# One filter product per unit on GpSimd, weight conversion wholly on VectorE, a conversion operation behind each filter unit, and the next item's stages one step later

## The chip, the cores and the metric

One core of a Trainium2 chip. The metric is the device time of one execution in microseconds (us), the median over several executions. PE is TensorE, DVE is VectorE, ACT is ScalarE, POOL is GpSimd, SP is SyncE, which only issues transfers here. L391 and the like are source lines; the changed kernel's lines stand up to 15 further down than the same lines before (the products of the plain steps are L609 before and L624 after).

## The reference

```python
X = np.fft.rfft(x, axis=1)                    # x: (8, 3008, 256)
Y = X * (filt_r + 1j * filt_i)[None]
y = np.fft.irfft(Y, n=3008, axis=1)           # then 24064 tokens of 256
h = y.reshape(24064, 256) @ w_in              # 256 -> 2048
g = h * np.clip(h + 3.0, 0.0, 6.0) / 6.0
out = g @ w_out                               # 2048 -> 256
```

The line that makes `g` is called the hardswish here.

## The kernel before

The transforms are written as matmuls in stages, and the feed-forward part as steps over blocks of 512 tokens, eight steps a block. From the second block on each product is done with seven instead of eight sub-products, which needs sums of weight blocks. The beginning has four stretches: loading and the first stage of batch item 0; its filter stage; the "direct" stage, which makes the first tokens; and the eight *plain steps* of the first block, which do without the weight sums. In the plain steps the weights are also converted: they are read as 64-bit words and turned into fp32 by integer and float operations, in 16 parts of 128x512, eleven of them within the plain steps, each shortly before the product that needs it. Some steps also hold a few *token products*, which make the tokens of a later stretch, and the first stage of batch item 1 runs beside the steps.

One filter unit, three products on VectorE:

```python
def f_unit(b, i):                       # cut
    if near(b, i):                      # b == 1, or b == 0 and i == NU - 2
        ...                             # four half products
    else:
        nc.vector.tensor_tensor(out=s1, in0=ps, in1=f, op=ALU.mult)
        nc.vector.tensor_tensor(out=s2[re], in0=ps[re], in1=f[im], op=ALU.mult)
        nc.vector.tensor_tensor(out=s2[im], in0=ps[im], in1=f[re], op=ALU.mult)
```

One conversion: six operations on VectorE, beside ScalarE's absolute value, and an end on VectorE (one operation) or on GpSimd (two):

```python
def w_conv(i, last):                    # cut
    v.tensor_scalar(out=big, in0=hi, ...)
    v.scalar_tensor_tensor(out=big, in0=hi, scalar=top_c, in1=big, ...)
    v.tensor_scalar(out=rest, in0=big, ...)
    v.tensor_scalar(out=lo, in0=lo, ...)
    v.scalar_tensor_tensor(out=rest, in0=lo.bitcast(FP32), scalar=1.0, in1=rest, ...)
    v.scalar_tensor_tensor(out=rest, in0=rest, scalar=2.0 ** -20, in1=big, ...)
    if last is v:
        v.scalar_tensor_tensor(out=w_part(i)[1], in0=two(high), scalar=least, in1=two(rest), ...)
    else:                               # GpSimd
        last.tensor_scalar(out=high, in0=high, scalar1=least, scalar2=None, op0=ALU.is_ge)
        last.tensor_tensor(out=w_part(i)[1], in0=two(high), in1=two(rest), op=ALU.mult)
```

The first stage of batch item 1 runs beside the steps. Its result goes through a pool of two buffers and is stored by SyncE for item 1, by GpSimd for later items; a block's output is stored by SyncE too, at the end of a step:

```python
t1p = pool("t1p", 2)
...
for c, s in enumerate(a_at):            # item 1: steps 2 to 9
    at(s, a_unit, n, c)                 # products; ScalarE copies them to a t1p buffer
    at(s, z_store, n, c, nc.sync if n == 1 else nc.gpsimd)
```

Of the kernel before, what the change touches and what calls it, by code (L numbers as in the profile page):

```python
# [10 lines left out]
FP32 = mybir.dt.float32  # L11
I32 = mybir.dt.int32
AXT = mybir.ActivationFunctionType
ALU = mybir.AluOpType
# [13 lines left out]
P = 128  # L28
# [6 lines left out]
NB = HC // XC  # L35
# [5 lines left out]
NU = KH // 2  # L41
# [73 lines left out]
def kernel(  # L115
# [9 lines left out]
    nc = tc.nc  # L125
# [14 lines left out]
    def pool(name, bufs, **kw):  # L140
        return ctx.enter_context(tc.tile_pool(name=name, bufs=bufs, **kw))
# [9 lines left out]
    rp = pool("rp", 2)  # L151
# [3 lines left out]
    op = pool("op", 2)  # L155
# [44 lines left out]
    def w_part(i):  # L200
        p = i // 2
        if i % 2 == 0:
            cols = ts(p, 256)
            src = moe_w_in[:, cols].bitcast(I32)
            return src.rearrange("(a p) d -> p a d", p=P), w_in[p][:, 0:4, :].rearrange("p (a j) m -> p a (j m)", a=2)
        src = moe_w_out[ts(p, 2 * P), :].bitcast(I32)
        return src.rearrange("(a p) d -> p a d", p=P), w_out[p][:, 0:4, :].rearrange("p (a j) m -> p a (j m)", a=2)
# [21 lines left out]
    def w_abs(i):  # L229
        words = st["bits", i].rearrange("p (n two) -> p n two", two=2)  # L230
        st["high", i] = sp.tile([P, 512], FP32, name="s1")
        nc.scalar.activation(out=st["high", i], in_=words[:, :, 1].bitcast(FP32), func=AXT.Abs)


    def w_conv(i, last):
        words = st.pop(("bits", i)).rearrange("p (n two) -> p n two", two=2)
        lo, hi = words[:, :, 0], words[:, :, 1]
        big, rest = (yp.tile([P, 2, D], FP32, name="y").bitcast(I32).rearrange("p a n -> p (a n)") for j in range(2))
        v = nc.vector
        high = st.pop(("high", i), None)  # L240
        v.tensor_scalar(out=big, in0=hi, scalar1=3, scalar2=0x3FFFFFFF,
                        op0=ALU.logical_shift_left, op1=ALU.bitwise_and)
        v.scalar_tensor_tensor(out=big, in0=hi, scalar=top_c, in1=big,
                               op0=ALU.bitwise_and, op1=ALU.bitwise_or)
        v.tensor_scalar(out=rest, in0=big, scalar1=23, scalar2=23,
                        op0=ALU.logical_shift_right, op1=ALU.logical_shift_left)
        v.tensor_scalar(out=lo, in0=lo, scalar1=9, scalar2=0x3F800000,
                        op0=ALU.logical_shift_right, op1=ALU.bitwise_or)
        if high is None:
            v.tensor_scalar(out=hi, in0=hi, scalar1=1, scalar2=1,  # L250
                            op0=ALU.logical_shift_left, op1=ALU.logical_shift_right)
            high = hi.bitcast(FP32)
        rest, big = rest.bitcast(FP32), big.bitcast(FP32)
        v.scalar_tensor_tensor(out=rest, in0=lo.bitcast(FP32), scalar=1.0, in1=rest,
                               op0=ALU.subtract, op1=ALU.mult)
        v.scalar_tensor_tensor(out=rest, in0=rest, scalar=2.0 ** -20, in1=big, op0=ALU.mult, op1=ALU.add)

        least = 1.125 * 2.0 ** -15
        two = lambda t: t.rearrange("p (a d) -> p a d", a=2)
        if last is v:  # L260
            v.scalar_tensor_tensor(out=w_part(i)[1], in0=two(high), scalar=least, in1=two(rest), op0=ALU.is_ge, op1=ALU.mult)
        else:
            last.tensor_scalar(out=high, in0=high, scalar1=least, scalar2=None, op0=ALU.is_ge)
            last.tensor_tensor(out=w_part(i)[1], in0=two(high), in1=two(rest), op=ALU.mult)

    def w_sums(i, late):
        w = (w_in, w_out)[i % 2][i // 2]
# [41 lines left out]
    def zt(dh):  # L309
        return (xn.rearrange("p a n -> p (a n)"), xs.rearrange("p i j d -> p (i j d)"))[dh]  # L310

    def copy(dve, to, ps):
        if dve:
            nc.vector.tensor_copy(out=to, in_=ps)
        else:
            nc.scalar.activation(out=to, in_=ps, func=AXT.Copy)
# [10 lines left out]
    def turn(c):  # L327
        t = t2p.tile([P, TC, D], FP32, name="t2")
        for v in range(2):
            ps = psU.tile([P, 512], FP32, name=("al", "be")[v])  # L330
            for u in range(2):
                for dh in range(2):
                    k = c * TC + 2 * v + u
                    nc.tensor.transpose(ps[:, ds(u * D + dh * P, P)], zt(dh)[:, ts(k, P)], st["start"][:, 0:P])
            copy(c == 0 and v == 1, t[:, 2 * v:2 * v + 2, :].rearrange("p k d -> p (k d)"), ps)
        st["t2", 0, c] = t
# [43 lines left out]
    def f_unit(b, i):  # L380
        c, r = divmod(2 * i, TC)
        ps = st.pop(("ps", b, i))
        f = st["ft", b, c][:, r:r + 2, :]

        pool_, n1, n2 = (hp, "h0", "h1") if b == 0 and i & 2 else (sp, "s1", "s2")
        s1, s2 = (pool_.tile([P, 512], FP32, name=n).rearrange("p (u d) -> p u d", u=2) for n in (n1, n2))

        re, im = slice(0, HALF), slice(HALF, P)
        if near(b, i):
            for s, part, to, x_ in (s1, re, re, re), (s1, re, im, im), (s2, im, re, im), (s2, im, im, re):  # L390
                nc.vector.tensor_tensor(out=s[to], in0=ps[x_], in1=f[part], op=ALU.mult)  # L391
        else:
# [3 lines that stand above are left out]
        st["y", b, i] = s1, s2  # L396


    def near(b, i):
        return b == 1 or b == 0 and i == NU - 2  # L400

    def y_unit(b, i):
        s1, s2 = st["y", b, i]
# [44 lines left out]
    for b in range(B):  # L448
        j = 0
        while j < HC:  # L450
            n = 1 if b == 0 and j == NJ else min(NJ, HC - j)
# [236 lines left out]
    with tc.manual_schedule():  # L688
# [22 lines left out]
        def convert(n):  # L711
            nonlocal done
            for i in range(n):
                w_conv(done, nc.vector)
                done += 1


        def convert_one():
            nonlocal done
            w_abs(done)  # L720
            w_conv(done, nc.gpsimd)
            done += 1
            load_bits(NCONV)

# [2 lines left out]
        ps = psU.tile([P, 512], FP32, name="al")  # L727
        for i in range(2):
            nc.tensor.matmul(ps, zero[:, P:2 * P], zero, start=True, stop=True)
        for j, n, bits in (0, 4, 0), (4, 4, 1), (8, 8, 1), (16, 8, 1), (24, 4, 1), (28, 4, 1):  # L730
            x0_load(j, n)
            load_bits(bits)
        table_load(0, 0)
# [9 lines left out]
        last = x0_at(HC * D - 2048, 3 * ND)  # L743
# [4 lines left out]
        nc.sync.dma_start(wai[:, 0:8, :], wai_d[:, 0:8, :])  # L748
        load_bits(4)
        turn(0)  # L750
        for c in range(NT):
            for i in (2 * c, 2 * c + 1):
                b_unit(0, i)
                f_unit(0, i)
                if c == NT - 1:
                    y_unit(0, i)
            if c + 1 < NT:
                turn(c + 1)
            if c:
                bi_unit(0, 2 * c - 2)  # L760
                (g0_first if c == NT - 1 else lambda i: g_store(0, i))(2 * c - 2)
            if c == 4:
                t4_load(0, 0, KH - 3 * TC, 1)
        t4_load(0, KH - 3 * TC, KH - TC, 1)
        for i in 1, 2:
            w_abs(i)
        direct(NU - 2)
        direct(NU - 1)
# [3 lines left out]
        bi_unit(0, NU - 2)  # L772
        for i in NU - 4, NU - 2:
            g_store(0, i)
        for i in 3, 4:
            w_abs(i)
        convert(4)
        for i in range(1, done):
            w_sums(i, False)

# [2 lines left out]

        at(0, x_load, 1, 0)

        for i, s in enumerate((0, 0, 1, 2, 2, 3, 4, 4, 5, 5, 6)):
            at(s, convert_one)
            at(s + 1, w_sums, done + i, False)
        for p in range(NP):
# [24 lines left out]
        def places(n):  # L814
            k = first[n]
            u = [NU - 1 - i for i in range(NU)]
            b_at = [(k - 2 - j // 3) * NP + 6 - 2 * (j % 3) for j in u]

            bi_at = [b_at[i] + (5 if i % 6 == 1 else 3) for i in range(NU)]
            a_at = [(k - 7 + c // 4) * NP + (0, 2, 5, 7)[c % 4] for c in range(NB)]  # L820
            if n == 1:
                a_at = list(range(2, NB + 2))
                b_at = [12, 13, 14, 18, 19, 20, 21, 22, 26, 27, 28, 29]
                bi_at = [i + 3 for i in b_at]
            return a_at, b_at, bi_at

        prev = None
        for n in range(1, B):
            a_at, b_at, bi_at = places(n)
# [7 lines left out]
            for c in range(NT):  # L837
                s = b_at[2 * (c - TB) + 1] + 1 if c >= TB else a_at[-1] + 1
                at(s, t2_load, n, c)
                s = b_at[2 * (c - FB) + 1] + 1 if c >= FB else a_at[-1 if n > 1 else 3] + 1  # L840
# [13 lines left out]
        for i in range(len(items) + 1):  # L854
            up = i < len(items)
            k, p = items[min(i, len(items) - 1)]
# [54 lines left out]
        k, v, add = NBLK - 1, nc.vector.tensor_tensor, ALU.add  # L911
# [37 lines left out]
```

## Time and profile before

| us | before |
|---|---|
| median of 4 runs | 2744.39 us (2740.41 to 2745.24) |
| span of the profiled run | 2739.3 us |
| filter products of the second pair start | 32.22 |
| first product of the plain steps | 69.74 |
| first product of the second block | 148.72 |
| a first-stage product of item 3 | 726.71 |

The last four rows are marks for a ledger. The filter products come in six *pairs* of units; a pair's start is its first product on TensorE. The profile of before is of one of its quicker runs (2741.46 us), which is why differences of 1 to 3 us are taken from runs of one chip together, and the profiles are used for where time goes.

### The profile page before, as it was taken

How to read it: one execution, taken by the hardware profiler on the slowest of the kernel's cores; microseconds unless marked ns; L12 is line 12 of the kernel's file. 1: busy time of each engine (PE TensorE's matmuls, PEld its weight loads, DVE VectorE, ACT ScalarE, POOL GpSimd, SP SyncE). 2: the span in 40 equal slices, each digit the busy share in tenths (PEclk: the TensorE clock that was granted, in tenths of full speed). 3: DMA queues.
4: the chain of work that ended last, by engine and by line, in shares of the span. 5: the costliest groups of instructions: out<-in, count | busy, mean ns of one | idle time of the engine just before them, and what ended most of it. 6: DMA issues, size and time to landing. Idle time of an engine off the chain costs nothing.

```text
span 2739.3 us, 47106 instructions
## 1 busy us (share of the span) xinstructions
PE 2701.9 (99%) x18100; PEld 2404.1 (88%) x18100; DVE 1955.4 (71%) x3383; ACT 1329.9 (49%) x2662; POOL 458.8 (17%) x646
## 2 busy tenths in 40 slices
PE   8899999999999999999999999999999999999998
PEld 6578889998899988999889998899988999999997
DVE  6868766787567875678756777577775777766665
ACT  3344455445544455444554445544455454545443
POOL 2833321101210012100121001210012100100000
PEclk9999999999999999999999999999999999999999
DMA  8642233221332123321233212332123321100000
GB/s 233 182 114 85 50 86 90 73 56 47 87 92 74 50 55 87 89 69 50 56 92 101 65 39 61 90 95 69 39 57 91 92 73 39 43 23 24 19 9 16
DMA packets 119644, 195.87 MB, mean 72 GB/s; under 512 B 21561, under 2 KB 82681, under 8 KB 119105
## 3 DMA queue, kind: packets, MB, share of 16 engines
q1 hardware_dynamic: 101627, 148.14, 19.1%
q0 software_dynamic: 17152, 44.23, 6.9%
q8 instruction: 143, 2.34, 0.4%
q14 instruction: 80, 0.66, 0.1%
q10 hardware_dynamic: 642, 0.51, 0.1%
HBM read 120.86 MB, written 71.93 MB: 70 GB/s over the span
## 4 chain that ended last, share of the span: by engine, by line
PE 93%; DVE 3%; DMA 2%; POOL 1%; issue 1%; ACT 0%; SPq 0%; POOLq 0%; DVEq 0%
PE po L598 42%; PE al L522 23%; PE be L522 17%; PE psn L476 4%; PE psf L376 3%; PE psf L353 2%; PE psf L423 2%; DVE s L391 1%; PE po L620 1%; DMA w_all<-in_x_dram 1%; DMA xs<-in_x_dram 0%; DVE g L572 0%; PE al L609 0%; DVE g L579 0%; PE po L376 0%
## 5 line engine op out<-in xcount | busy, mean ns | idle before, releaser
L598 PEld LDWEIGHTS po<-w_all,g 128*128 128x128 f32 x10304 | 1368.2, 191 | 142.1 <-issue 38.1
L598 PE MATMUL po<-w_all,g 128*128 128x128 f32 x10304 | 1399.3, 276 | 0.8 <-DVE g L572 0.6
L572 DVE SCALAR_TENSOR_TENSOR g<-r,h 128x512 f32<-128x512 f32 x736 | 511.9, 696 | 275.6 <-ACT r L567 263.9
L567 ACT ACTIVATE r<-h,half_c 128x512 f32<-128x512 f32 x736 | 531.1, 722 | 329.9 <-DVE h L548 317.9
L522 PE MATMUL al<-xt,w_all 128*128 128x256 f32 x2208 | 660.4, 381 | 3.8 <-DVE h L553 3.3
L522 PE MATMUL be<-xn,w_all 128*128 128x256 f32 x1472 | 437.8, 379 | 0.0
L548 DVE TENSOR_TENSOR h<-be,s 128x512 f32<-128x512 f32 x368 | 254.1, 690 | 252.9 <-PE be L522 241.7
L522 PEld LDWEIGHTS al<-xt,w_all 128*128 128x128 f32 x2208 | 335.3, 192 | 6.4 <-DVE h L553 4.7
L522 PEld LDWEIGHTS be<-xn,w_all 128*128 128x128 f32 x1472 | 279.7, 190 | 37.9
L562 ACT ACTIVATE h<-al 128x256 f32<-128x256 f32 x368 | 141.4, 384 | 347.9 <-PE al L522 347.9
L553 DVE TENSOR_TENSOR h<-al,s 128x256 f32<-128x256 f32 x368 | 156.2, 424 | 164.5 <-PE al L522 163.2
L580 DVE TENSOR_TENSOR g<-g 128x512 f32<-128x512 f32 x368 | 257.2, 699 | 12.6
L543 ACT ACTIVATE s<-al 128x256 f32<-128x256 f32 x368 | 141.4, 384 | 198.3 <-PE al L522 198.3
L534 ACT ACTIVATE s<-be 128x256 f32<-128x256 f32 x368 | 141.4, 384 | 176.3 <-PE be L522 176.3
L522 PE MATMUL al<-xn,w_all 128*128 128x256 f32 x736 | 219.9, 381 | 0.5 <-ACT h L562 0.5
L522 PE MATMUL be<-xt,w_all 128*128 128x256 f32 x736 | 218.9, 379 | 0.0
L365 POOL DMA_DIRECT2D z_tmp<-t x192 | 110.7, 581 | 414.6 <-ACT t L356 412.4
L533 ACT ACTIVATE s<-al 128x256 f32<-128x256 f32 x368 | 141.4, 384 | 71.0 <-PE al L522 70.9
L579 DVE TENSOR_TENSOR g<-g 128x256 f32<-128x256 f32 x368 | 162.5, 441 | 12.6
L582 DVE TENSOR_TENSOR g<-g 128x256 f32<-128x256 f32 x368 | 161.0, 438 | 12.5
L654 POOL TENSOR_TENSOR o<-p,o 128x256 f32<-128x256 f32 x45 | 32.7, 728 | 794.1 <-ACT t L426 366.4
L522 PEld LDWEIGHTS be<-xt,w_all 128*128 128x128 f32 x736 | 139.8, 190 | 18.9
(143 smaller groups left out, 1944.3 us busy)
## 6 DMA issues: line engine op xcount, KB each, us to landing
g_tmp<-t POOLq DMA_DIRECT2D x96, 256.0 KB, 3.8
t<-g_tmp SPq DMA_DIRECT2D x188, 120.0 KB
t<-z_tmp SPq DMA_DIRECT2D x42, 512.0 KB
z_tmp<-t POOLq DMA_DIRECT2D x192, 96.0 KB, 3.2
out_dram<-o SPq DMA_DIRECT2D x321, 47.0 KB
xs<-in_x_dram SPq DMA_DIRECT2D x112, 128.0 KB
ft<-in_filt_r_dram SPq DMA_DIRECT2D x88, 128.0 KB
ft<-in_filt_i_dram SPq DMA_DIRECT2D x88, 128.0 KB
```

The costliest lines, as they stand in the source:

```text
L522: nc.tensor.matmul(ps, w_in[p][:, w, :], x, start=start, stop=stop, skip_group_check=True)
L533: nc.scalar.activation(out=s[:, 0, :], in_=al, func=AXT.Copy)
L534: nc.scalar.activation(out=s5, in_=be[:, 1, :], func=AXT.Copy)
L543: nc.scalar.activation(out=s[:, 1, :], in_=al, func=AXT.Copy)
L548: nc.vector.tensor_tensor(out=st["h"][0].rearrange("p (a n) -> p a n", a=2), in0=be, in1=s, op=ALU.add)
L553: nc.vector.tensor_tensor(out=st["h"][1][:, 256:512], in0=al, in1=s5, op=ALU.add)
L567: nc.scalar.activation(out=r, in_=st["h"][i], func=AXT.Relu, bias=half_c, scale=1.0 / 6.0)
L572: nc.vector.scalar_tensor_tensor(out=st["g", k, p][:, o:o + 2, :].rearrange("p a n -> p (a n)"), in0=st["r", i], scalar=1.0, in1=st["h"][i ...
L579: v.tensor_tensor(out=g[:, G1, :], in0=g[:, G3, :], in1=g[:, G22, :], op=ALU.add)
L580: v.tensor_tensor(out=g[:, G3:G2 + 1:2, :], in0=g[:, G3:G1 + 1, :], in1=g[:, G11:G11 + 1, :].broadcast_to([P, 2, 256]), op=ALU.subtract)
L582: v.tensor_tensor(out=g[:, G4, :], in0=g[:, G12, :], in1=g[:, G2, :], op=ALU.subtract)
L598: nc.tensor.matmul(st["po", k][bank][:, part, u, :], g[:, a, ts(u, P)], w_out[p][:, w, :], start=(p == 0 and n in OPENS and u == 0), stop= ...
```

## The change

The intent: in the plain steps GpSimd and VectorE are both nearly full with conversions, and TensorE waits for them. GpSimd's share goes to VectorE; VectorE is relieved earlier, in the filter stage, where GpSimd has little to do: GpSimd makes one of three products there, from a copy by ScalarE, and VectorE does the second conversion between the units.

```diff
-        if near(b, i):
+        if b == 0:
+            xf = rp.tile([P, 512], FP32, name="r", tag="r").rearrange("p (u d) -> p u d", u=2)
+            nc.scalar.activation(out=xf, in_=ps, func=AXT.Copy)
+            nc.gpsimd.tensor_tensor(out=s1, in0=xf, in1=f, op=ALU.mult)
+            nc.vector.tensor_tensor(out=s2[re], in0=ps[re], in1=f[im], op=ALU.mult)
+            nc.vector.tensor_tensor(out=s2[im], in0=ps[im], in1=f[re], op=ALU.mult)
+        elif near(b, i):
...
-        return b == 1 or b == 0 and i == NU - 2
+        return b == 1
...
+        between = w_ops(1)              # the conversion as a generator, one operation at a time
+        next(between)
         for c in range(NT):
             for i in (2 * c, 2 * c + 1):
                 b_unit(0, i)
                 f_unit(0, i)
+                next(between, 0)
...
-        convert(4)                      # before the plain steps
+        convert(3)
...
-        for i, s in enumerate((0, 0, 1, 2, 2, 3, 4, 4, 5, 5, 6)):   # later conversions, by step
+        for i, s in enumerate((0, 1, 1, 2, 3, 3, 4, 4, 5, 5, 6)):   # their end on VectorE now
...
-                a_at = list(range(2, NB + 2))        # item 1, first stage, by step
-                b_at = [12, 13, 14, 18, ...]
+                a_at = list(range(3, NB + 3))
+                b_at = [13, 14, 15, 18, ...]
```

Besides, the first weight load trades places with an x load (cut here).

More of the change, by code (lines that the diff above doesn't have):

```diff
@@ L232, in w_abs, with w_conv, w_ops @@
         nc.scalar.activation(out=st["high", i], in_=words[:, :, 1].bitcast(FP32), func=AXT.Abs)
-    def w_conv(i, last):
+    def w_conv(i):
+        for _ in w_ops(i):
+            pass
+    def w_ops(i):
         words = st.pop(("bits", i)).rearrange("p (n two) -> p n two", two=2)
@@ L242, in w_conv @@
                         op0=ALU.logical_shift_left, op1=ALU.bitwise_and)
+        yield
         v.scalar_tensor_tensor(out=big, in0=hi, scalar=top_c, in1=big,
                                op0=ALU.bitwise_and, op1=ALU.bitwise_or)
+        yield
         v.tensor_scalar(out=rest, in0=big, scalar1=23, scalar2=23,
                         op0=ALU.logical_shift_right, op1=ALU.logical_shift_left)
+        yield
         v.tensor_scalar(out=lo, in0=lo, scalar1=9, scalar2=0x3F800000,
                         op0=ALU.logical_shift_right, op1=ALU.bitwise_or)
+        yield
         if high is None:
@@ L252, in w_conv @@
             high = hi.bitcast(FP32)
+            yield
         rest, big = rest.bitcast(FP32), big.bitcast(FP32)
@@ L255, in w_conv @@
                                op0=ALU.subtract, op1=ALU.mult)
+        yield
         v.scalar_tensor_tensor(out=rest, in0=rest, scalar=2.0 ** -20, in1=big, op0=ALU.mult, op1=ALU.add)
-        least = 1.125 * 2.0 ** -15
+        yield
         two = lambda t: t.rearrange("p (a d) -> p a d", a=2)
-        if last is v:
-            v.scalar_tensor_tensor(out=w_part(i)[1], in0=two(high), scalar=least, in1=two(rest), op0=ALU.is_ge, op1=ALU.mult)
-        else:
-            last.tensor_scalar(out=high, in0=high, scalar1=least, scalar2=None, op0=ALU.is_ge)
-            last.tensor_tensor(out=w_part(i)[1], in0=two(high), in1=two(rest), op=ALU.mult)
+        v.scalar_tensor_tensor(out=w_part(i)[1], in0=two(high), scalar=1.125 * 2.0 ** -15, in1=two(rest),
+                               op0=ALU.is_ge, op1=ALU.mult)
+        yield
     def w_sums(i, late):
@@ L713, in convert @@
             for i in range(n):
-                w_conv(done, nc.vector)
+                w_conv(done)
                 done += 1
@@ L720, in convert_one @@
             w_abs(done)
-            w_conv(done, nc.gpsimd)
+            w_conv(done)
             done += 1
@@ L729 @@
             nc.tensor.matmul(ps, zero[:, P:2 * P], zero, start=True, stop=True)
-        for j, n, bits in (0, 4, 0), (4, 4, 1), (8, 8, 1), (16, 8, 1), (24, 4, 1), (28, 4, 1):
+        for j, n, bits in (0, 4, 0), (4, 4, 0), (8, 8, 1), (16, 8, 1), (24, 4, 1), (28, 4, 1):
             x0_load(j, n)
@@ L764 @@
         t4_load(0, KH - 3 * TC, KH - TC, 1)
-        for i in 1, 2:
+        done = 2
+        for i in 2, 3:
             w_abs(i)
@@ L774 @@
             g_store(0, i)
-        for i in 3, 4:
-            w_abs(i)
-        convert(4)
+        w_abs(4)
+        convert(3)
         for i in range(1, done):
@@ L821, in places @@
             if n == 1:
-                a_at = list(range(2, NB + 2))
-                b_at = [12, 13, 14, 18, 19, 20, 21, 22, 26, 27, 28, 29]
+                a_at = list(range(3, NB + 3))
+                b_at = [13, 14, 15, 18, 19, 20, 21, 22, 26, 27, 28, 29]
                 bi_at = [i + 3 for i in b_at]
```

## The prediction

> **What bounds the kernel now.** I read the page first, then the busy times by stretch, then the waits of the stretch in which TensorE loses time, then single rows of its timeline.
>
> ```profile
> span 2739.3 us, 47106 instructions
> ...
> PE 2701.9 (99%) x18100; PEld 2404.1 (88%) x18100; DVE 1955.4 (71%) x3383; ACT 1329.9 (49%) x2662; POOL 458.8 (17%) x646
> ...
> PE 93%; DVE 3%; DMA 2%; POOL 1%; issue 1%; ACT 0%; SPq 0%; POOLq 0%; DVEq 0%
> ```
>
> TensorE is 99% busy and is 93% of the chain that ended last. The change only touches the beginning and leaves TensorE's instructions alone, so all that can be won is time that TensorE loses there. The steps over 512-token blocks begin at 69.74 us with the first block's plain products; its eight steps run to 148.72, where the first product of the second block starts. From there to the end are 2590 us of TensorE work that the change does not shorten. The stretches are the filter stage, the "direct" stage, and the eight plain steps:
>
> ```profile
> core 0: us, PE busy (x) PEld busy (x) DVE busy (x) ACT busy (x) POOL busy (x), PEclk, DMA share, GB/s
> 28.00:57.00 29.00, 25.94 (x134) 16.08 (x132) 26.14 (x38) 11.89 (x21) 7.26 (x10) 1.00 0.99 289
> 57.00:69.74 12.74, 12.36 (x65) 7.98 (x65) 12.02 (x23) 2.82 (x7) 1.24 (x2) 1.00 0.70 178
> 69.74:148.72 78.98, 69.42 (x247) 39.71 (x245) 67.21 (x91) 27.40 (x45) 71.27 (x82) 0.91 0.68 190
> ```
>
> In the last row VectorE (67.2 of 79.0) and GpSimd (71.3) are both nearly full: they convert weights, block by block, just ahead of the products. TensorE is idle 79.0 - 69.4 = 9.6 us, and its clock is 0.91, so about 0.09 x 79 = 7 us more go in slow matmuls: 16.6 us lost in all. The waits of this stretch name the causes:
>
> ```profile
> PE al L609 <- DVE g L572: 4.3, 1, 4.3
> ...
> PE al L609 <- POOL w_all L264: 3.0, 1, 3.0
> ...
> PE psf L353 <- DMA xs<-in_x_dram: 2.3, 1, 2.3
> ```
>
> The first waits for a hardswish that stands on VectorE behind the last of four conversions, the second for the last operation of a conversion, which GpSimd does. Each is followed by slow matmuls (the reader compares the group of four products, 3.78 us after the wait, 1.88 in the next step):
>
> ```profile
> 77.75 3.78 PE L609 MATMUL al<-xn,w_all 128*128 128x512 f32 x4 [4.31 <-DVE g L572]
> ...
> 87.79 1.88 PE L609 MATMUL al<-xn,w_all 128*128 128x512 f32 x4
> ```
>
> **What the Trainium skill says.** "SBUF — State Buffer", section "Who interferes with whom": a VectorE instruction with two SBUF inputs, or in a two-port mode, contends with a GpSimd instruction that reads SBUF, and the one that comes second waits the other out; with at most one SBUF input, outside such a mode, it does not. This trace agrees:
>
> ```profile
> 54.27 1.26 POOL L408 TENSOR_TENSOR r<-h,h 64x512 f32<-64x512 f32 x1 [1.17 <-DVE h L391]
> ...
> 54.93 0.69 DVE L393 TENSOR_TENSOR h<-po,w_all 128x512 f32<-128x512 f32 x1
> ...
> 82.57 1.33 POOL L264 TENSOR_TENSOR w_all<-s,y 128x512 f32<-128x512 f32 x1 [0.54 <-DVE y L256]
> ...
> 82.80 1.66 DVE L243 SCALAR_TENSOR_TENSOR y<-bits,top_c,y 128x512 int32<-128x512 int32 x1
> ```
>
> L243 costs 0.75 alone, but 1.66 when it starts 0.2 us into L264; the filter product L393, with one input in PSUM, keeps its 0.69 beside GpSimd's work. "TensorE: Matmul & The Clock Gate", section "What's actually happening", says that the array falls to half clock after an idle window of some 3.4 us and needs as long a busy time to return: the 3.78 above agrees. "GPSIMD Engine Reference", section "1. Specifications": GpSimd has no PSUM access, hence the ScalarE copy in the change.
>
> **The change part by part.**
>
> 1. Filter units (12). Of three VectorE products of 0.69 us one goes (8.3 us of VectorE in all). It comes back as a ScalarE copy (0.60, as the other 128x512 PSUM copies) and a GpSimd product (1.30, as L264). VectorE per pair of units: 4 x 0.71 = 2.85 instead of 4.3. Behind units 0 to 6 stands one operation of the second conversion each (0.42 to 0.75, mean 0.57), one more ahead. TensorE's own period per pair is 4.67 us (its filter products start at 32.22, 36.85, 41.52, 46.18, 50.85, with no idle gap worth naming), so this stage is TensorE-bound and nothing is won in it. VectorE's new load per pair is 2.85 + 1.2 = 4.1, plus up to 1 us each time a conversion operation meets a GpSimd product: 4.1 to 6.1 around 4.67. ScalarE: 6 x 0.60 = 3.6. GpSimd: 2 x 1.30 + 1.13 for the store's issue = 3.7. All fit, VectorE barely. I expect 0 to 1.5 us of delay. The first weight load only trades places with an x load: the same bytes lie ahead of the filter tables that start this stage, so nothing changes.
>
> 2. Last pair. GpSimd made both sums before (2 x 1.26, ready at 56.86). Now VectorE does (2 x 0.69), but behind GpSimd's product, itself behind a store's issue (51.98 to 53.1): product to 54.4 or 54.7; and the sum, with two SBUF inputs, may wait out the next product, to 56.0. So ready at 55.9 to 57.4: from 1 us won to 0.5 lost. Together with part 1 I take a start of the direct stage and of the plain steps about 0.5 us late (70.2 instead of 69.7).
>
> 3. VectorE between filter and hardswish. Before: from 58.5 four conversions of 4.18 us (58.52 to 62.70 for one), the last slowed, first hardswish at 77.00. Now three: 60.2 (57.4, then two products and two sums of 0.7 for the last unit) + 3 x 4.18 = 72.7. TensorE finishes the first step's products at 70.2 + 3.45 = 73.65, and the hardswish it waits for ends at 73.5. The wait of 4.31 and the slow matmuls after it (3.78 + 3.0 instead of 1.72 + 1.72, so 3.3) go: 7.6 us.
>
> 4. Eleven later conversions. GpSimd loses L263 (1.66) and L264 (1.30): 11 x 2.96 = 32.6 of its 71.3 us. VectorE gains one operation: 11 x 0.72 = 7.9. It gets back part of the interference: the six operations take 3.40 alone, but by the group means of this stretch 0.56 + 1.00 + 0.74 + 0.77 + 0.82 + 0.85 = 4.74. With GpSimd half empty and the 1.3 us blocks gone I estimate 4.4 for seven (5.1 while the sums of four parts run).
>
> 5. VectorE then becomes the pacer of the plain steps. Walking it: hardswish pair (1.2) to 75.1; conversion to 80.2; pair to 81.4; two conversions (step 1 now has two) to 90.3. TensorE is ready for that hardswish at 87.9 and waits until 90.9: 3 us, and I allow 2 for slow clock. After this the two run level (two conversions and a pair 10.0 us, a TensorE step 8.1, those with token products 9.2, steps with one conversion 5.6). TensorE's eight steps need 3.45 + 7 x 7.0 + 2 x 1.1 (token products) + 5 x 1.02 (first-stage products) = 59.8 without waits. 70.2 + 59.8 + 3 + 2 = 135.0, against 148.72: 13.7 us. The wait for L264 (3.0 + 1.5 slow) and, as the x load gets one step more time, the 2.3 + 2.4 for xs are in this sum.
>
> 6. First-stage products start one step later, so one of them (1.02) moves behind the eight steps: it is work moved, not removed. 13.7 - 1.0 = 12.7. Rounded for small waits that I cannot see: 12. 2744.06 - 12 = 2732.
>
> **The rivals.**
>
> *VectorE takes the place of GpSimd.* From 56 us to the end of the plain steps it has 4 sums (2.8), 14 conversions (58.5 unimpeded) and 16 hardswishes (9.7): 71 us; with 6 to 12 us of interference, 133 to 139. For it: 67.2 of 79 us busy already, 0.72 us added per conversion. If conversions cost 5.0 instead of 4.4, the end moves by 11 x 0.6 = 6.6: 2738.
>
> *The weight loads or SyncE's queue become the bound.* ScalarE waited 2.8 and 2.6 us for weight bits, and the last loads stand behind x loads that wait for TensorE. Against: a buffer is free a conversion and a hardswish pair (5.6 us) before its next use and a load takes about 4.2 (124.81 to 128.95). Worth 2 to 4 us: 2735.
>
> *The filter stage gets slower,* because conversion operations and GpSimd's products hold each other up. At the worst, seven blocks of 1 us less the slack: 3 us, so 2735.
>
> *All goes right:* no stall before the fourth step, so 130 + 1 - 148.7, about 18 us: 2727.
>
> **Range and chances.** Everything at stake is under 20 us, 0.7% of the time, and a doubled interference still gains a few. 8 in 10: 2726 to 2740. Faster or slower than 2% (55 us) would need something outside the beginning: 0.01 and 0.005.
>
> **What would show it.** In the profile after: plain steps' clock near 1.0 and TensorE idle under 5 us; the second block's first product at 133 to 137; no L263/L264 work, GpSimd busy about 38 us in the plain steps; the first hardswish near 73; filter products still 4.67 apart; a TensorE wait for a hardswish in the fourth plain step. Wrong if the filter products are over 5 us apart, if conversions stay at 5 us, or if waits for weight bits appear.

## The result, and the profile after

The changed kernel takes 2744.62 us (4 runs, 2742.87 to 2745.02) against 2744.39. The ratio is 1.0002, 95% interval 0.9985 to 1.002: no change, where 12 us less were predicted. All ratios here are the mean time of one kernel's runs over that of the other's of the same rounds, so they are not quite the ratios of the medians that are quoted. Executions over 1.5% slower than the fastest of the same kernel are left out of the means.

The first view is the busy time by stretch of the changed kernel: filter stage, direct stage, plain steps, and what follows them. The columns are those of the prediction's table.

```profile
27.30:57.00 29.70, 26.11 (x128) 15.95 (x128) 27.36 (x31) 16.38 (x31) 18.97 (x19) 1.00 0.87 260
57.00:73.46 16.46, 14.19 (x66) 8.93 (x64) 15.69 (x25) 4.37 (x10) 2.44 (x3) 0.90 0.69 192
73.46:142.06 68.60, 64.04 (x238) 37.24 (x237) 61.28 (x96) 25.74 (x42) 39.45 (x65) 0.98 0.64 180
142.06:200.00 57.94, 50.59 (x315) 43.26 (x314) 26.51 (x44) 24.50 (x50) 4.00 (x5) 0.94 0.38 102
```

In the third row is what was hoped for: the plain steps take 68.6 us instead of 79.0, TensorE's clock there is 0.98 instead of 0.91, and GpSimd is busy 39.5 instead of 71.3 us. But they start at 73.46 instead of 69.74, and in the last row TensorE is idle for 57.94 - 50.59 = 7.3 us at a clock of 0.94. In the kernel before the stretch behind the plain steps looks like this:

```profile
148.72:200.00 51.28, 49.65 (x318) 43.35 (x317) 30.92 (x49) 23.91 (x49) 9.36 (x13) 1.00 0.29 85
```

There it is idle 1.6 us at full clock. The ledger, from the marks of both profiles:

| stretch | before | after | difference |
|---|---|---|---|
| to the second pair of filter products | 32.22 | 31.72 | -0.5 |
| from there to the plain steps | 37.52 | 41.74 | +4.2 |
| plain steps | 78.98 | 68.60 | -10.4 |
| from there to the mark at 726.71 or 730.61 | 577.99 | 588.55 | +10.6 |
| sum | 726.71 | 730.61 | +3.9 |

So most of the expected gain came, and was given back in two places. The waits of TensorE from 142 us on name the second one; each row is who waited, on whom, the us in total, how often and the longest:

```profile
ACT t L364 <- DMA z_tmp<-t: 7.8, 1, 7.8
PE al L537 <- ACT s L558: 6.8, 2, 6.3
```

TensorE waits for a copy by ScalarE, and ScalarE, which in this trace runs its copies in the order of the program, stands before another copy (L364, a first-stage result of item 1) that needs a buffer whose store has not landed. SyncE's issues and the two waiting instructions in order of time:

```profile
139.74 1.56 SPq L373 DMA_DIRECT2D z_tmp<-t  x4
...
149.20 12.50 SPq L690 DMA_DIRECT2D out_dram<-o  x14
161.75 9.25 SPq L373 DMA_DIRECT2D z_tmp<-t  x12
```

```profile
168.34 1.08 ACT L364 ACTIVATE t<-psf 128x512 f32<-128x512 f32 x2 [7.76 <-DMA z_tmp<-t]
```

```profile
169.85 1.19 PE L537 MATMUL al<-xt,w_all 128*128 128x256 f32 x2 [6.27 <-ACT s L558]
```

There are two buffers. The sixth result was copied at 144.64, but its store stands behind the 14 issues that store the first block's output, 12.5 us of SyncE's time, and is issued at 161.75. The eighth result, at 161, needs that buffer. In the kernel before, everything was one step earlier: the sixth store was issued ahead of the output stores, at 146.39 against 155.79:

```profile
146.39 1.61 SPq L365 DMA_DIRECT2D z_tmp<-t  x4
155.79 11.88 SPq L675 DMA_DIRECT2D out_dram<-o  x14
```

Two matmuls of L537 at 169.85 take 1.19 us where 0.60 is usual: the clock is down after the wait.

The other place is the filter stage. VectorE's and GpSimd's timelines there, both of the changed kernel:

```profile
37.78 0.69 DVE L403 TENSOR_TENSOR h<-po,ft 64x512 f32<-64x512 f32 x1
38.51 3.09 DVE L258 TENSOR_SCALAR bits<-bits 128x512 int32<-128x512 int32 x1
41.63 0.68 DVE L402 TENSOR_TENSOR s<-po,w_all 64x512 f32<-64x512 f32 x1
42.34 0.69 DVE L403 TENSOR_TENSOR s<-po,w_all 64x512 f32<-64x512 f32 x1
43.07 3.25 DVE L263 SCALAR_TENSOR_TENSOR y<-bits,y 128x512 f32<-128x512 f32 x1
```

```profile
37.41 1.37 POOL L455 DMA_DIRECT2D g_tmp<-t  x2 [1.12 <-ACT t L441]
38.69 2.61 POOL L401 TENSOR_TENSOR s<-r,w_all 128x512 f32<-128x512 f32 x2
42.06 1.18 POOL L455 DMA_DIRECT2D g_tmp<-t  x2 [0.76 <-ACT t L441]
43.17 2.58 POOL L401 TENSOR_TENSOR h<-r,w_all 128x512 f32<-128x512 f32 x2
```

L258, a conversion operation, takes 0.42 us alone and 3.09 here; L263 takes 0.69 alone and 3.25. Both end a little after the second of two GpSimd products: 38.69 + 2.61 = 41.30, and L258 ends at 41.60; 43.17 + 2.58 = 45.75, and L263 ends at 46.32, that is 0.57 later. Two earlier ones are lengthened less, by 0.9 us each (L248, 1.65; L251, 1.34). The filter products around them (one input in PSUM) keep their 0.68. The store issues that GpSimd makes in between do not do it: in e2 (below) L258 ran wholly inside such an issue (37.45, the issue from 36.84 to 38.20) and took 0.43, while three later operations of 1.93, 3.01 and 3.20 us ended 0.55 to 0.57 us after the second of two products. TensorE then waits for VectorE:

```profile
47.79 1.07 PE L438 MATMUL psf<-s,wi 128*64 128x512 f32 x2 [2.04 <-DVE s L403]
```

The fourth pair of filter products starts at 41.02, the next at 48.79: 7.8 us apart where the prediction counted on 4.67; over 5 us was one of its own signs of being wrong.

The predicted wait in the fourth plain step is there as well, to a tenth, with its slow matmuls (3.32 where 1.88 is usual). The conversions ahead of it took 5.1 and 8.9 us, as the prediction had walked them:

```profile
94.51 3.32 PE L624 MATMUL al<-xn,w_all 128*128 128x512 f32 x4 [2.93 <-DVE g L587]
```

### The profile page after: what moved, and what is told of

The parts are those of the page before. It is cut to its first block, busy times and chain, and to the rows that moved or that the text cites. A ratio compares the mean times of both kernels' runs of the same rounds, so it can differ in the third digit from the quotient of the medians.

```text
span 2743.2 us, 47103 instructions
## 1 busy us (share of the span) xinstructions
PE 2701.6 (98%) x18100; PEld 2403.2 (88%) x18100; DVE 1954.4 (71%) x3384; ACT 1335.9 (49%) x2673; POOL 437.1 (16%) x634
## 4 chain that ended last, share of the span: by engine, by line
PE 93%; DVE 4%; DMA 1%; issue 1%; ACT 0%; POOL 0%; SPq 0%; POOLq 0%; DVEq 0%; ACTq 0%
PE po L613 41%; PE al L537 23%; PE be L537 17%; PE psn L491 4%; PE psf L384 2%; PE psf L361 2%; PE psf L438 2%; DVE s L406 1%; DVE g L587 1%; DMA w_all<-in_x_dram 0%; DVE y L263 0%; DMA out_dram<-o 0%; DVE g L594 0%; PE psn L512 0%; DVE y L248 0%
## 5 line engine op out<-in xcount | busy, mean ns | idle before, releaser
L537 PE MATMUL al<-xt,w_all 128*128 128x256 f32 x2208 | 661.4, 381 | 9.0 <-ACT s L558 6.8
L537 PE MATMUL be<-xn,w_all 128*128 128x256 f32 x1472 | 437.8, 379 | 0.0
L537 PEld LDWEIGHTS al<-xt,w_all 128*128 128x128 f32 x2208 | 335.7, 192 | 11.5 <-issue 9.1
L537 PEld LDWEIGHTS be<-xn,w_all 128*128 128x128 f32 x1472 | 279.7, 190 | 37.9
L537 PE MATMUL al<-xn,w_all 128*128 128x256 f32 x736 | 219.9, 381 | 0.5 <-ACT h L577 0.5
L537 PE MATMUL be<-xt,w_all 128*128 128x256 f32 x736 | 218.9, 379 | 0.0
L597 DVE TENSOR_TENSOR g<-g 128x256 f32<-128x256 f32 x368 | 161.0, 438 | 12.5
L537 PEld LDWEIGHTS be<-xt,w_all 128*128 128x128 f32 x736 | 139.8, 190 | 18.9
```

Source lines behind the costliest of these rows:

```text
L537: nc.tensor.matmul(ps, w_in[p][:, w, :], x, start=start, stop=stop, skip_group_check=True)
L597: v.tensor_tensor(out=g[:, G4, :], in0=g[:, G12, :], in1=g[:, G2, :], op=ALU.subtract)
```

## The experiments

Eleven runs, five timed rounds each, in three sets; the runs of a set share a chip and the runs of the kernel before.

| run | median us | before, same chip | ratio (95%) |
|---|---|---|---|
| e1 stores by GpSimd | 2739.49 | 2742.59 | 0.9989 (0.9976 to 1.0003) |
| e2 steps put back | 2735.66 | 2742.59 | 0.9974 (0.9961 to 0.9986) |
| e3 conversion alone | 2734.25 | 2742.59 | 0.9973 (0.9961 to 0.9986) |
| e4 step shift alone | 2750.72 | 2742.59 | 1.0033 (1.002 to 1.0046) |
| e5 GpSimd product alone | 2736.60 | 2744.48 | 0.9971 (0.9959 to 0.9984) |
| e6 interleaving alone | 2737.68 | 2744.48 | 0.9977 (0.9964 to 0.9989) |
| e7 even units | 2734.46 | 2744.48 | 0.9965 (0.9952 to 0.9977) |
| e8 even units, places | 2733.33 | 2744.48 | 0.9963 (0.9949 to 0.9976) |
| e9 changed kernel again | 2746.60 | 2743.61 | 1.0012 (0.9998 to 1.0026) |
| e10 e1 again | 2739.32 | 2743.61 | 0.9986 (0.9973 to 0.9999) |
| e11 all three repairs | 2734.07 | 2743.61 | 0.9965 (0.9953 to 0.9978) |

### The late wait: e1, e2, e4, and e9 with e10

e1, and e10 again:

```diff
-                at(s, z_store, n, c, nc.sync if n == 1 else nc.gpsimd)
+                at(s, z_store, n, c, nc.sync if n == 1 and c < 5 else nc.gpsimd)
```

> The changed kernel, but the first-stage stores of the second batch item from the sixth on are issued by GpSimd instead of SyncE. Theory QUEUE (the plain steps did get 10 us shorter, and 8 us of it were given back at 163 us, where ScalarE waits for a buffer whose store stands behind the first block's 14 output stores on SyncE's queue): TensorE's wait of 6.3 us for ScalarE's copy and the slow matmuls after it go, 2744.6 becomes 2736 to 2738. Rival CHANCE (that wait belongs to DMA traffic in general and comes somewhere else): within 2 us of 2744.6.

e2, the changed kernel with the steps of before:

```diff
-                a_at = list(range(3, NB + 3))
-                b_at = [13, 14, 15, 18, ...]
+                a_at = list(range(2, NB + 2))
+                b_at = [12, 13, 14, 18, ...]
```

> The changed kernel, but with the first and second stages of the second batch item at the steps at which the kernel before had them (one step earlier). QUEUE: the sixth store is again ahead of the output stores, so the wait at 163 us goes: 2736 to 2739 (one first-stage product of 1 us comes back into the plain steps, and the x load may be late by up to 2 us). CHANCE: within 2 us of 2744.6.

e4, the same two lines changed the other way in the kernel before, and nothing else:

> The kernel before with nothing but the one-step shift of the second item's first and second stages. QUEUE: the sixth store lands behind the output stores here too, TensorE waits about 6 us some 20 us after the second block's first product: 2744 becomes 2749 to 2753 (less up to 4.7 us if the late x load no longer stops TensorE in the fourth plain step). CHANCE: within 2 us, or a little faster by the x load's 4.7 us.

In e1 and e2 the wait at 163 us is gone, and e4 has it, without any other part of the change (the wait comes later there, as the second block starts at 146.38):

```profile
173.40 1.09 ACT L356 ACTIVATE t<-psf 128x512 f32<-128x512 f32 x2 [8.57 <-DMA z_tmp<-t]
```

e2 came out 0.3 us below its range; e4 lost 8.1 us, within its own. e1 missed its range by 1.5 us, which left open whether the size was off or the comparison with another chip; so the changed kernel and e1 were run once more side by side.

> The changed kernel itself, once more, on the same chip as the next two. If the difference of e1 to it (5 us where 8.3 were expected) came from comparing two chips, the next run is 7 to 9 us below this one; if the late wait was dearer in the one profile than it is in most executions, 4 to 6 us.

> e1 once more, beside the changed kernel on one chip: 7 to 9 us below e9 by QUEUE with the profile's size, 4 to 6 if the size was off, under 2 by CHANCE.

On one chip e10 is 2746.60 - 2739.32 = 7.3 us faster than e9, in the range for QUEUE. In e10 GpSimd issues the sixth result's store at 147.14, before SyncE's output stores, which start at 150.33:

```profile
147.14 2.38 POOL L373 DMA_DIRECT2D z_tmp<-t  x4 [3.69 <-ACT s L558]
```

The profiles also show where e1's missing 1.5 us may lie. In e1, e9 and e10 the filter stage cost more than in the first profile of the changed kernel, with the same wait of 2.04 us: from the second pair to the plain steps 43.4 to 43.5 us instead of 41.7. e9 is the same program as the changed kernel, and its eight products behind that wait took 3.68 us instead of 1.99, at a granted clock of 0.57 instead of 1.00 (49 to 53 us):

```profile
48.15 1.07 PE L438 MATMUL psf<-s,wi 128*64 128x512 f32 x2 [2.04 <-DVE s L403]
49.15 3.68 PE L384 MATMUL po<-t,w_all 128*128 128x256 f32 x8
```
The marks agree: from the second block's first product to the mark in item 3 the changed kernel takes 588.55 (588.58 in e9), e10 takes 723.48 - 143.19 = 580.29, e2 takes 721.29 - 143.22 = 578.07, the kernel before 577.99. So of the 10.6 us that the shift cost behind the plain steps, 8.3 are the wait and its slow clock, and 2.3 remain when the stores do not queue. The first-stage product that moved out of the plain steps is 1.0 of these; TensorE's idle time is 0.6 longer in e10 than in e2 (5.97 against 5.36 us; e10 has a wait of 1.80 us for a hardswish 67 us into the second block that e2 has not, and fewer short ones); the rest is not traced. CHANCE is refuted.

### The parts: e3, e5, e6

e3 has of the change only VectorE's conversions, their places and the traded load: filter units, sums and steps are those of before.

```diff
-        between = w_ops(1)
-        next(between)
...
-                next(between, 0)
...
-        w_abs(4)
-        convert(3)
+        for i in 3, 4:
+            w_abs(i)
+        convert(4)
```

(and the three-product unit, its sums and a_at, b_at as before)

> The kernel before's filter products (three on VectorE), no conversion operations between them, the kernel before's steps for the second item; of the change only the conversion wholly on VectorE with its places. Theory PARTS (conversion on VectorE saves some 6 to 8 us, the filter part costs 4, the step shift costs 8): plain steps start at 69.7 again, the second block's first product at 141 to 143, 2736 to 2739. Rival VECTORE-BOUND (the fourth conversion in front of the first hardswish keeps its wait and VectorE never catches up): second block's first product at 147 or later, 2743 or more.

PARTS held, a little better than its range: 0.9973, 8.3 us below before, with the second block's first product at 141.15. The one part saves 8.3 of the 12 us that were hoped from the whole. The first hardswish still makes TensorE wait 4.31 us, as before.

e5 is e2 with the same edit as above but GpSimd's product kept; e6 is e2 with VectorE making all three products and the operations left between the units.

> e2 (changed kernel with the steps put back), but the second conversion goes back behind the filter stage whole: GpSimd's product stays, nothing stands between the units on VectorE. Theory LOCK (a conversion operation that starts beside GpSimd's product waits that product and the next one out, 3.1 us instead of 0.4 to 0.7, twice in this stage): filter products 4.67 us apart all through, no VectorE operation over 1 us before the last pair, the direct stage some 3 us earlier than in e2, but the fourth conversion is back ahead of the first hardswish; total 2733 to 2737. Rival TRANSFER (the ScalarE copy and the GpSimd product themselves come late for TensorE): a gap of 3 us in the filter products stays.

> e2 without GpSimd's product: VectorE does all three products of a unit and the conversion operations stand between the units. LOCK: no conversion operation over 0.8 us there; VectorE's sum per pair is 4.3 + 1.2 = 5.5 us against TensorE's 4.67, so TensorE falls behind by up to 3 us, but by work and not by blocked operations; total 2734 to 2738. Rival LOAD (the long operations come from VectorE's own queue or from the transfers into SBUF at that time): operations of 2 to 3 us appear here too.

In e5 no VectorE operation of the filter stage is over 1 us until the last pair, though GpSimd makes its products two in a row as in the changed kernel, and the filter products from the third pair on start 4.66 or 4.67 us apart:

```profile
37.30 1.99 PE L384 MATMUL po<-t,w_all 128*128 128x256 f32 x8
41.96 1.99 PE L384 MATMUL po<-t,w_all 128*128 128x256 f32 x8
46.63 1.99 PE L384 MATMUL po<-t,w_all 128*128 128x256 f32 x8
51.29 0.92 PE L384 MATMUL po<-t,w_all 128*128 128x256 f32 x3
```

So neither the copy nor the product is late: TRANSFER is refuted. (The direct stage came only 1.5 us earlier than in e2, counted from the second pair, not 3: the second pair ran at a slow clock after a 1.9 us wait for a table.) In e6, without GpSimd's product, the very operations that took 3 us are short:

```profile
40.01 0.43 DVE L258 TENSOR_SCALAR bits<-bits 128x512 int32<-128x512 int32 x1
...
42.62 0.69 DVE L263 SCALAR_TENSOR_TENSOR y<-bits,y 128x512 f32<-128x512 f32 x1
```

LOAD is refuted; the long operations need both the products on GpSimd and the operations on VectorE. As LOCK said, e6 is late by work alone: its direct stage starts 28.7 us after the second pair (60.36 - 31.70), against 24.7 before (56.92 - 32.22) and 27.9 in the changed kernel.

### Placing the operations: e7, e8, e11

e7, on e2:

```diff
-        if b == 0:
+        if b == 0 and i % 2 == 0:
             xf = ...                     # GpSimd's product
...
-        next(between)
...
-                next(between, 0)
+                if i % 2:
+                    next(between, 0)
+                    next(between, 0)
```

> e2, but GpSimd makes the product of the even units alone and two conversion operations stand behind each odd unit, so that by the order of the units GpSimd has finished when they start. VectorE per pair: 5 x 0.71 + 2 x 0.57 = 4.7, as TensorE's 4.67. LOCK: conversion operations 0.4 to 0.8 us, filter products 4.67 apart, plain steps start near 69 instead of 72 to 73, with three conversions ahead of the first hardswish; total 2731 to 2734. Rival: blocked operations of 2 us and more stay, 2735 or more.

It came to 2734.46, 0.5 us above LOCK's range and 0.5 below the rival's, with a spread of 8 us over its runs. The profile answers in part only. TensorE kept its 4.67 us all through (32.07, 36.73, 41.40, 46.06, 50.73), but one operation was still blocked for 2.02 us:

```profile
49.41 2.02 DVE L266 SCALAR_TENSOR_TENSOR y<-y 128x512 f32<-128x512 f32 x1
```

```profile
48.39 1.18 POOL L455 DMA_DIRECT2D g_tmp<-t  x2 [3.49 <-ACT t L441]
49.51 1.36 POOL L401 TENSOR_TENSOR s<-r,w_all 128x512 f32<-128x512 f32 x1
```

It met the tail of a store's issue and then one product, and ended 0.56 us after it (51.43 against 50.87), as the others ended after two. The plain steps started at 71.94, not near 69.

e8, on e7:

```diff
-        for i, s in enumerate((0, 1, 1, 2, 3, 3, 4, 4, 5, 5, 6)):
+        for i, s in enumerate((0, 1, 2, 2, 3, 3, 4, 4, 5, 5, 6)):
```

> e7, with the third of the eleven later conversions one step later (one conversion each in the first and second plain steps, then two). Theory: the wait of 2.9 us for the hardswish of the third step comes from two conversions standing ahead of it on VectorE, and goes with its slow matmuls; 3 to 5 us less than e7: 2726 to 2730. Rival (VectorE's total bounds the plain steps wherever the conversions stand): the wait moves to a later step and the time stays within 1.5 us of e7.

The wait of the fourth plain step is gone in e8's profile, and waits of 0.8 and 2.1 us appear in the seventh and eighth. The times are 1.1 us apart, which is the rival's range, but the profiled runs' plain steps are 69.2 (e8) and 72.9 us (e7), and e7's contain 2.7 us of a late x load that e8's do not. The theory's 2726 to 2730 was missed, and both things that the rival said came (within 1.5 us, the wait in later steps), so this points to the rival; with e7's spread of 8 us it does not settle it. VectorE is busy for 62.4 of 69.2 us in e8's plain steps, so little is likely left to win by moving conversions.

> The changed kernel with all three repairs: GpSimd's product for even units alone with two conversion operations behind each odd unit, the third later conversion one step later, and the first-stage stores from the sixth on by GpSimd, so that the second item's steps can stay one later. Against e8 (steps put back): the x load has more time, but one first-stage product moves from the plain steps into the next ones, which fits as well. Expected 0.995 to 0.997 of the kernel before, that is within 3 us of e8's 2733; if the late wait comes back, 2740 or more.

e11 is 2734.07, ratio 0.9965, as expected: the later steps of the change can stay if the stores do not queue behind the output. Against the kernel before on their own chips e3, e5, e7, e8 and e11 save 8 to 11 us, e2 and e6 7. That is under 0.5%, but these intervals lie wholly below 1; among themselves they overlap, and the runs are not told apart.

## Why the prediction was wrong

- **The bound.** Right for what could be won: TensorE's losses in the beginning, 16.6 us in the plain steps. But the time behind 148.72 was taken as fixed, and there step 6 failed. (The best case is a slip: 2744.06 less 17.7 is 2726.4, not 2727; nothing rests on it.)
- **Step 1, the filter units.** This step failed on size: "up to 1 us each time a conversion operation meets a GpSimd product", "I expect 0 to 1.5 us of delay". The mechanism was the one it named. But a blocked operation waited until the second of two products had ended, 3.1 and 3.25 us, not for one product. The direct stage started 3.2 us later after the second pair than before (27.87 against 24.70), and slow matmuls behind TensorE's next wait made 4.2 of it by the plain steps (5.9 in e9's profile of the same program). e5 and e6 show that the pair of causes is needed. The third rival, with "seven blocks of 1 us less the slack: 3 us", had the size, though mainly from two long blocks (2.7 and 2.6 us too long) and not from seven short ones.
- **Step 2, the last pair.** Right: the sum on VectorE that meets the other unit's product took 1.76 instead of 0.69 us.
- **Step 3, the first hardswish.** Right: the 4.31 us wait and its slow matmuls are gone (second step's products at 77.00, directly behind the first's).
- **Step 4, the conversions.** A size that was off: 4.4 us each was my estimate; the eleven took 4.8 on average (52.7 us together, counted from first operation to first operation of what follows), as VectorE's operations still run beside GpSimd's sums of weight blocks, and not only those with two SBUF inputs: L254, with one, takes 0.42 alone and 0.68 beside a sum (90.93, the sums from 89.29 to 91.32). Some 4 us of VectorE's time.
- **Step 5, the plain steps.** The wait of 3 us in the fourth step: measured 2.93. The stretch took 68.6 us where my sum gave 64.8: a further wait of 1.36, and first-stage products that take 1.7 instead of 1.02 right behind a token product (as rows of the kernel before already showed), are parts of that.
- **Step 6, the shifted steps.** This step failed outright: "it is work moved, not removed", 1.0 us. The shift put the sixth store behind the output stores, and a wait of 6.3 us with its slow clock took the place of those removed; 8.3 us by the marks, and e4 has them without the rest. The second rival named SyncE's queue, but for the weight loads and at 2 to 4 us; I never asked behind which other transfers a store would come to stand and when its buffer is needed again.

Predicted were +0.5, -14.2 and +1.0; measured +4.2, -10.4 and +10.6, with -0.5 from the loading. With the steps put back (e2) the kernel takes 2735.66, inside the predicted range; that is 6.9 us below before on its chip, where 12 were predicted, so step 1 and the smaller terms cost the rest. With the steps kept and only the stores moved (e10) it is 4.3 us below before, at the edge of the range. So step 6 decided the miss, and step 1 alone would have used up about a third of the gain.

What stays open: why GpSimd's second product goes ahead of a VectorE operation that already waits (in the plain steps, beside GpSimd's short sums, an operation of VectorE was lengthened by up to 0.5 us); and the loading, whose end moves the first filter products between 26.2 and 29.0 us over these profiles and with them the times of one kernel by some us.

## What to carry to other kernels

When a stage is moved by a step, follow its stores: find what stands ahead of them on the same issuing engine, when their buffers are needed again, and which engine works in order behind that wait. When work is given to GpSimd to relieve VectorE, look at what VectorE does beside it: here its operations with one PSUM input were untouched, and short ones from SBUF to SBUF took up to seven times their length. And a change of several parts is worth splitting even when its sum is zero: here one part was worth 8 us.

## What the Trainium skill lacked or had wrong

- "SBUF — State Buffer", "Who interferes with whom": the page has the loser wait for the whole instruction of the other. Here a waiting VectorE operation let two whole GpSimd products of 1.3 us go by (3.09 and 3.25 us for operations of 0.42 and 0.69), so the cost per meeting is not bounded by one instruction. In the profile these VectorE operations even start 0.1 to 0.2 us before the first of the two products (GpSimd's times are rough). The rest of the rule held in the filter stage of every run that was looked at: single products with an input in PSUM never took over 0.70 us.
- "TensorE: Matmul & The Clock Gate", "Why this matters for your kernels", tells in its table to avoid idle gaps of more than about 3 us. Shorter gaps were followed by slow matmuls here in some executions and not in others: after the same 2.04 us eight matmuls took 1.99 us in one profile of the changed kernel and 3.68 in another (e9); after 2.27 us four matmuls took 2.21 us in the changed kernel, after 2.23 us they took 1.81 in e2; after 2.11 us in e8 four others took 3.39 instead of 1.88.
- "DMA: Bandwidth & Descriptors", "Issuing engines are not separate DMA queues", calls the issue time that a second engine saves usually small. Here it was the point: 14 issues took SyncE 12.5 us, and three results' stores issued by GpSimd instead saved 7.3 us (e10 against e9). I found no page that says that a store which only waits to be issued holds its buffer as long (here from 144.64 to 168.34 us).
